# The first four cells of a fused mLSTM and feed-forward kernel: exponents by bias, scaling on GpSimd, and cell 4 turned within the first product group

## The chip, the cores and the metric

The kernel runs on one core of one Trainium2 chip. The metric is the device time of one execution in microseconds; before the change the median of three runs is 540.57 us (540.18 to 541.71). The profile is of one further execution, whose span is 539.1 us.

## The reference

An mLSTM cell goes over 768 time steps for 4 batches and 8 heads with head dimension 40; its output, seen as 3072 rows of 320, goes through a feed-forward block whose activation is h times cos(h). All in float32.

```python
for t in range(S):
    m_new = np.maximum(f_gate[:, :, t] + m, i_gate[:, :, t])
    f_stab, i_stab = np.exp(f_gate[:, :, t] + m - m_new), np.exp(i_gate[:, :, t] - m_new)
    C = f_stab * C + i_stab * outer(vt, kt);  n = f_stab * n + i_stab * kt     # per batch and head
    y[:, :, t] = sigmoid(o_gate) * (C @ qt) / np.maximum(np.abs(n @ qt), 1.0)
...
h = x @ w_in            # 3072x320 by 320x2048
return (h * np.cos(h)) @ w_out
```

## The kernel before

**Tiling.** Time is cut into 6 chunks of 128 steps; with 4 batches that makes N = 24 *cells*, numbered n = 4c + b. Within a cell the recurrence is written as attention with decay. `turn` transposes q and k on TensorE and `turn_out` copies them out of PSUM. `scores` multiplies them, and `weigh` (VectorE, L451) multiplies the scores by E, the decay matrix of 128 x 1024. `values` multiplies the result by v, giving ph. `normalize` divides by the denominator (dn, L533 to L535), multiplies by the gate (y, L538) and writes the scaled z in the order of the feed-forward (L542 and L546). `seam` transposes z on TensorE into px and forms the cell's contribution pu to the state (with kw from `weigh_k`, k weighed by gates on GpSimd, L392). `seam_out` copies px to xT and `state` adds pu to the state, both on ScalarE for the first four cells.

**E.** It is exp of minus (M spread over rows, minus a per-row number from `tab`), masked to the lower triangle. `decay_exponents` subtracts on VectorE (L370) and masks on GpSimd (L371) before `decay` takes the exponential on ScalarE in one instruction (L379). `decay_by_bias` (L381 to L387) instead gives ScalarE the per-row number as bias, which takes one instruction for each of the 8 heads (L385), and masks on GpSimd afterwards (L386). Cells 0 and 1 have a third way, by products on TensorE (`wall_in`, `spread`, `decay_exponents_half`).

**Staging.** `first_cells` (L760 to L872) writes out by hand the order of the first four cells, which have no feed-forward beside them. The order of a call in the program is its order in the queue of its engine: each of TensorE, VectorE, ScalarE, GpSimd and the queue of transfers on SyncE works strictly through its own list. Then `both_parts(c, b)` runs for every chunk c and batch b: the feed-forward of chunk c in eight `Up` groups (h for 256 columns of w_in, and cosine by range reduction and ScalarE's Sin) and `down` groups, with the cells of chunk c + 1 between them. The first `Up` needs xT of all four cells, so it follows `seam_out(3)`.

**Weights.** The weights come as 8-byte floats and are turned to float32 in pieces: `parts` on ScalarE (L138, L140), `join` on VectorE (L144, L146, L148) with a last addition on GpSimd (L149), or on VectorE where a caller says so. The first three pieces are joined within `first_cells`.

**Fillers.** `warm(k)` issues k products of a zero tile, 128 x 512 in bfloat16, which keep TensorE active.

**Buffers.** z and y have one buffer each. In PSUM, cells 0 and 2 use a ring of two buffers (`ps_a`), cells 1 and 3 one of four (`ps_o`).

**The gates.** `gates_first` computes the running maximum M0 of the first chunk and writes it to DRAM (L223); `load_E(2)` and `load_E(3)` read it back, spread over 128 rows, and stand in the queue of SyncE behind that write. `gates_less_sums` (L242) subtracts 32 x 640 elements for the later chunks, ahead of the scan in `gates_maxima` (L247).

Of the kernel before, what the change touches and what calls it, by code (L numbers as in the profile page):

```python
# [16 lines left out]
OP = mybir.AluOpType  # L17
# [12 lines left out]
def kernel(  # L30
# [20 lines left out]
    nc = tc.nc  # L51
# [165 lines left out]
    def gates_first():  # L217
        nc.vector.tensor_tensor_scan(out=F0, data0=one.to_broadcast([BH, C]), data1=F0, initial=0.0,
                                     op0=OP.mult, op1=OP.add)
        nc.vector.tensor_tensor(out=a0, in0=a0, in1=F0, op=OP.subtract)  # L220
        nc.vector.tensor_tensor_scan(out=M0, data0=one.to_broadcast([BH, C]), data1=a0, initial=-1.0e30,
                                     op0=OP.mult, op1=OP.max)
        nc.gpsimd.dma_start(out=M_d[0], in_=M0)  # L223
        nc.vector.tensor_scalar(out=nM, in0=M0[:, C - 1:C], scalar1=-1.0, scalar2=None, op0=OP.mult)
        nc.scalar.activation(out=e0, in_=a0, func=AF.Exp, bias=nM)

    def gates_first_out():
        pg = ps_o.tile([128, 2, BH], FP, name="pg", tag="o")
        for j, src in enumerate((a0, e0)):
            nc.tensor.transpose(pg[:, j], src, ident[0:BH, 0:BH])  # L230
        nc.vector.tensor_copy(out=tab[:, 0, 0:2], in_=pg)
# [7 lines left out]
        nc.vector.tensor_tensor_scan(out=flat[0], data0=flat[3], data1=flat[0], initial=0.0, op0=OP.mult, op1=OP.add)  # L239

    def gates_less_sums():
        nc.vector.tensor_tensor(out=a1, in0=a1, in1=F1, op=OP.subtract)  # L242
        nc.vector.tensor_copy(out=shift[:, 0, 0:1], in_=F0[:, last])
        nc.vector.tensor_copy(out=shift[:, 1:R, 0:1], in_=F1[:, 0:R - 1, last])

# [92 lines left out]
    def load_E(n):  # L338
        c, b = divmod(n, B)
        E = p4.tile([128, H, C], FP, name="E", tag="E")  # L340
        if n not in SPREAD:
            src = M_d[0][ts(b, H)] if c == 0 else M_d[1][ts(b, H), ts(c - 1, C)]
            nc.sync.dma_start(out=E, in_=src.unsqueeze(0).to_broadcast([128, H, C]))
        Es[n] = E
# [33 lines left out]
    def decay(n):  # L378
        nc.scalar.activation(out=Es[n], in_=Es[n], func=AF.Exp, scale=-1.0)  # L379
# [9 lines left out]
    def weigh_k(n):  # L389
        if n < N - B:  # L390
            kw = p2.tile([128, H, D], FP, name="kw", tag="kw")
            nc.gpsimd.tensor_tensor(out=kw, in0=ks[n % NB][:, :, 0:D], in1=cols(n, 1, D), op=OP.mult)  # L392
            kws[n] = kw
# [128 lines left out]

    def normalize(n):
        c, b = divmod(n, B)
        pq, hs = heads_of[n]
        if n >= B:
            ph = hs
            hs = p1.tile([128, H, D1], FP, name="hs", tag="hs")
            nc.vector.tensor_tensor(out=hs, in0=pq, in1=cols(n, 2, D1), op=OP.mult)
            nc.vector.tensor_tensor(out=hs, in0=hs, in1=ph, op=OP.add)  # L530
        dn = p2.tile([128, H], FP, name="dn", tag="dn")

        nc.vector.scalar_tensor_tensor(out=dn, in0=hs[:, :, D], scalar=-TWO_PI, in1=least, op0=OP.mult, op1=OP.max)  # L533
        nc.vector.scalar_tensor_tensor(out=dn, in0=hs[:, :, D], scalar=TWO_PI, in1=dn, op0=OP.mult, op1=OP.max)
        nc.vector.reciprocal(out=dn, in_=dn)  # L535
        y = p1.tile([128, H, D], FP, name="y", tag="y")
        o = sig[c][:, ts(b, DM)].rearrange("t (h d) -> t h d", h=H)
        nc.vector.tensor_tensor(out=y, in0=o, in1=hs[:, :, 0:D], op=OP.mult)  # L538

        z = p1.tile([128, DM + 64], FP, name="z", tag="z")  # L540
        za = z[:, 0:NK * 128].rearrange("t (i k d) -> t k i d", i=2, k=HP)
        nc.vector.tensor_tensor(out=za, in0=y[:, :, 0:DA].rearrange("t (k i) d -> t k i d", i=2),  # L542
                                in1=dn.rearrange("t (k i) -> t k i", i=2).unsqueeze(3).to_broadcast([128, HP, 2, DA]),
                                op=OP.mult)
        shape = [128, 2, H, DL]
        nc.vector.tensor_tensor(out=z[:, NK * 128:].rearrange("t (e h d) -> t e h d", e=2, h=H),  # L546
                                in0=y[:, :, DA:D].unsqueeze(1).to_broadcast(shape),
                                in1=dn.unsqueeze(1).unsqueeze(3).to_broadcast(shape), op=OP.mult)
        ys[n] = z
# [51 lines left out]
    class Up:  # L601


        def __init__(self, c, f2):
            self.c, self.f2 = c, f2
            self.pu = [ps_u.tile([128, B * C], FP, name="pup", tag="up") for _ in range(2)]

            def x(i, r=slice(0, 128)):
                return xT[c][r, i].rearrange("p b t -> p (b t)")

            for i in range(NK):
                for e, pu in enumerate(self.pu):
                    nc.tensor.matmul(pu, w_in_sb[:, i, ts(block(f2, e), 128)], x(i), start=(i == 0), stop=False)  # L613
            for e, pu in enumerate(self.pu):
                r = slice(64 * e, 64 * e + 64)
                nc.tensor.matmul(pu, w_in_l[r, f2], x(NK, r), start=False, stop=True)  # L616
            self.n = [p3.tile([128, B * C], I32, name="n", tag="n") for _ in range(2)]
# [137 lines left out]
    def warm(k, bank=None):  # L755

        for _ in range(k):
            nc.tensor.matmul(bank or pw, nil, nil.unsqueeze(1).to_broadcast([128, HP, 128]), start=True, stop=True)

    def first_cells():  # L760
        nc.vector.memset(nil, 0.0)
        gates_in()
        nc.scalar.copy(out=ident_b, in_=ident)
        load(0, "qk")
        later_gates_in()
        load(1, "qk")
        load(0, "v")
        load_o(0, (0, 1))
        load(2, "qk")
        load_E(0)  # L770
        load_E(1)
        warm(12)
        wall_in(0, 0, pmu)
        wall_in(0, 1, psum_o())
        gates_first()
        gates_first_out()
        spread(0, 0)
        decay_exponents_half(0, 0)
        turn(0)
        turn_out(0, False)  # L780
        gates_sums()
        spread(0, 1)
        decay_exponents_half(0, 1)
        decay(0)
        weigh_k(0)
        load_E(2)
        load(1, "v")
        load(3, "qk")
        load_o(0, (2, 3))
        load_E(3)  # L790
        load(2, "v")
        load(3, "v")
        pieces.extend(weights_in(0))
        wall_in(1, 0, psum_o())
        wall_in(1, 1, psum_o())
        gates_less_sums()
        spread(1, 0)
        decay_exponents_half(1, 0)
        scores(0)
        gates_maxima()  # L800
        turn(1)
        weigh(0)
        sigmoid(0, slice(0, 2))
        turn_out(1, False)
        spread(1, 1)
        decay_exponents_half(1, 1)
        gates_exponents()
        decay(1)
        weigh_k(1)
        values(0)  # L810
        normalize(0)
        scores(1)
        gates_exp()
        turn(2)
        turn_out(2, False)
        warm(2)
        seam(0)
        weigh(1)
        seam_out(0)
        state(0)  # L820
        load(B)
        decay_exponents(2)
        gates_diagonal()
        decay(2)
        weigh_k(2)
        values(1)
        load_E(B)
        load_o(1, (0,))
        load_E(B + 1)
        outs.append((0, weights_out(0)))  # L830
        normalize(1)
        scores(2)
        turn(3)
        sigmoid(0, slice(2, 4))
        seam(1)
        weigh(2)
        decay_exponents(3)
        turn_out(3)
        seam_out(1)
        values(2)  # L840
        decay(3)
        weigh_k(3)
        state(1)
        normalize(2)
        scores(3)
        pg = gates_turn()
        warm(1)
        seam(2)
        weigh(3)
        join(*parts(*pieces.pop(0)))  # L850
        pieces.extend(weights_in(1))
        load(B + 1)
        outs.extend((p, weights_out(p)) for p in range(1, 3))
        load_o(1, (1, 2, 3))
        seam_out(2)
        join(*parts(*pieces.pop(0)))
        state(2)
        gates_keep(*pg)
        values(3)
        normalize(3)  # L860
        turn(B)
        warm(3)
        seam(3)
        join(*parts(*pieces.pop(0)), nc.vector)
        seam_out(3)
        decay_exponents(B)
        load_E(B + 2)
        state(3)
        turn_out(B, False)
        decay(B)  # L870
        weigh_k(B)
        sigmoid(1, slice(0, 1))  # L872
# [17 lines left out]
    def both_parts(c, b):  # L890
# [6 lines left out]
        begin = c == b == 0  # L897
        more = cell and n + 1 < N
        f2 = 2 * b
        up = Up(c, f2)  # L900
        if cell:
            scores(n)
            if begin:
# [144 lines left out]
```

## Time and profile before

| | |
|---|---|
| time, median of 3 | 540.57 us |
| TensorE (PE) busy | 529.1 us, 98% of the span |
| VectorE (DVE) busy | 368.6 us, 68% |
| ScalarE (ACT) busy | 262.1 us, 49% |
| GpSimd (POOL) busy | 166.9 us, 31% |
| transpose of z of cell 0 / 1 / 2 / 3 begins | 19.04 / 23.98 / 29.48 / 37.02 us |
| transposes of q and k of cell 4 begin | 33.80 us |
| first / second `Up` begins | 38.52 / 49.16 us |

The busy shares are averages over the whole span. The change lies in the first 45 us, so the rows of the timeline matter more: a start in us from the beginning of the span, a duration, the engine, the line, what is written and read, and in brackets how long the engine had been idle and for what. PEclk is the share of full clock that TensorE was granted.

### The profile page before, as it was taken

Reading aid. Unit: us, or ns where it says so; the run is one execution under the profiler, and the core shown is the slowest. Engines: PE = TensorE matmul, PEld = TensorE weight load, DVE = VectorE, ACT = ScalarE, POOL = GpSimd, SP = SyncE. Lnnn points to the kernel's source line nnn. Section 1 sums busy time; section 2 is a strip of 40 time slices with the busy share of each in tenths; the row PEclk is TensorE's granted clock in tenths of the full one; section 3 lists DMA queues with packets and bytes.
Section 4 is the critical chain, followed back from the end, with each engine's and each line's share of the span. In section 5 each row is a group of like instructions: output and inputs, shape, how many; then the busy total and the mean of one; then the engine's idle time right before and its main releaser. Section 6 shows DMA issues by size and latency. Waiting matters only on the chain.

```text
span 539.1 us, 9945 instructions
## 1 busy us (share of the span) xinstructions
PE 529.1 (98%) x3635; PEld 334.4 (62%) x3635; DVE 368.6 (68%) x727; ACT 262.1 (49%) x415; POOL 166.9 (31%) x304
## 2 busy tenths in 40 slices
PE   9989899999999999999999999999999999999997
PEld 6865556665566666656656656756656656656555
DVE  5876987968777767777767777776876765522323
ACT  4868695866543436525427425327335332322312
POOL 5531333426353652322422422322222221212121
PEclk9979999999999999999999999999999999999999
DMA  9999996744166744076724075635065000010001
GB/s 140 207 203 217 252 234 174 155 115 83 47 141 144 157 97 84 23 165 143 153 76 107 4 183 139 143 83 117 5 158 117 21 16 11 6 49 0 2 0 49
DMA packets 134512, 56.86 MB, mean 105 GB/s; under 512 B 72080, under 2 KB 130528, under 8 KB 134464
## 3 DMA queue, kind: packets, MB, share of 16 engines
q1 hardware_dynamic: 134320, 56.04, 46.8%
q8 instruction: 28, 0.46, 0.4%
q0 software_dynamic: 96, 0.18, 0.2%
q14 instruction: 20, 0.16, 0.1%
q10 hardware_dynamic: 48, 0.02, 0.0%
HBM read 50.00 MB, written 6.21 MB: 104 GB/s over the span
## 4 chain that ended last, share of the span: by engine, by line
PE 85%; DVE 4%; SPq 4%; DMA 4%; POOL 1%; ACT 1%; issue 1%; DVEq 0%; POOLq 0%
PE po L689 32%; PE pup L613 29%; PE pup L616 9%; PE po L746 4%; PE hp L488 3%; PE ps L445 3%; PE hp L482 2%; SPq L129 1%; PE pu L580 1%; DMA bits<-in_moe_w_in_dram 1%; DMA o<-in_o_gate_dram 1%; SPq L327 1%; DMA qs<-in_q_dram 1%; DVE wt L146 1%; PE pt L426 1%; DMA M_d<-M_rows 1%
## 5 line engine op out<-in xcount | busy, mean ns | idle before, releaser
L613 PE MATMUL pup<-xT,w_in_sb 128*128 128x512 f32 x384 | 175.6, 600 | 0.9 <-POOL w_in_sb L149 0.6
L621 ACT ACTIVATE n<-pup 128x512 int32<-128x512 f32 x96 | 52.1, 594 | 213.4 <-PE pup L616 213.4
L624 DVE SCALAR_TENSOR_TENSOR n<-pup,n 128x512 f32<-128x512 f32 x96 | 61.8, 686 | 119.9 <-ACT n L621 119.9
L689 PE MATMUL po<-w_out_sb,g 128*128 128x320 f32 (+1 forms) x480 | 118.6, 396 | 0.0
L613 PEld LDWEIGHTS pup<-xT,w_in_sb 128*128 128x128 f32 x384 | 70.0, 191 | 73.9 <-issue 61.9
L689 PEld LDWEIGHTS po<-w_out_sb,g 128*128 128x128 f32 x480 | 83.5, 190 | 36.7 <-issue 9.1
L672 POOL TENSOR_TENSOR sg<-g 128x128 f32<-128x128 f32 x80 | 36.6, 457 | 192.7 <-DVE g L633 191.2
L629 ACT ACTIVATE n<-n 128x512 f32<-128x512 f32 x96 | 58.8, 630 | 12.1 <-DVE n L624 12.1
L633 DVE SCALAR_TENSOR_TENSOR g<-pup,n 128x512 f32<-128x512 f32 x96 | 61.7, 685 | 2.5 <-ACT n L629 1.2
L616 PE MATMUL pup<-xT,w_in_l 64*128 64x512 f32 x192 | 54.2, 641 | 0.0
L371 POOL TENSOR_SCALAR_AFFINE_SELECT E<-E 128x1024 f32<-128x1024 f32 x19 | 20.7, 1091 | 104.4 <-DVE E L370 83.4
L689 PE MATMUL po<-T,sg 128*128 128x160 f32 x240 | 39.4, 300 | 0.0
L746 PE MATMUL po<-w_out_sb,g 128*128 128x320 f32 x128 | 36.6, 439 | 1.3 <-POOL w_out_sb L149 1.0
L616 PEld LDWEIGHTS pup<-xT,w_in_l 64*128 64x128 f32 x192 | 14.4, 184 | 36.4 <-issue 35.6
L689 PEld LDWEIGHTS po<-T,sg 128*128 128x128 f32 x240 | 34.8, 190 | 0.2
L451 DVE TENSOR_TENSOR E<-ps,E 128x512 f32<-128x512 f32 x48 | 30.7, 680 | 5.6 <-PE ps L445 5.6
L410 DVE STREAM_TRANSPOSE t<-qs 128x512 f32<-128x512 f32 x32 | 32.8, 1101 | 0.0
L445 PEld LDWEIGHTS ps<-t,t 40*128 40x128 f32 (+1 forms) x384 | 25.0, 188 | 9.7 <-issue 8.9
L746 PEld LDWEIGHTS po<-w_out_sb,g 128*128 128x128 f32 x128 | 23.7, 190 | 11.0 <-POOL w_out_sb L149 1.3
L379 ACT ACTIVATE E<-E 128x1024 f32<-128x1024 f32 x21 | 22.2, 1058 | 16.9 <-POOL E L371 15.7
L445 PE MATMUL ps<-t,t 40*128 40x128 f32 (+1 forms) x384 | 25.8, 274 | 0.0
L370 DVE TENSOR_TENSOR E<-E,tab 128x1024 f32<-128x1024 f32 x19 | 23.1, 1215 | 0.5 <-DMA E<-M_d 0.5
(146 smaller groups left out, 647.2 us busy)
## 6 DMA issues: line engine op xcount, KB each, us to landing
E<-M_d SPq DMA_DIRECT2D x22, 512.0 KB
bits<-in_moe_w_in_dram SPq DMA_DIRECT2D x40, 128.0 KB
bits<-in_moe_w_out_dram SPq DMA_DIRECT2D x8, 640.0 KB
room<-G_d SPq DMA_DIRECT2D x32, 128.0 KB
ks<-in_k_dram SPq DMA_DIRECT2D x24, 160.0 KB
vs<-in_v_dram SPq DMA_DIRECT2D x24, 160.0 KB
qs<-in_q_dram SPq DMA_DIRECT2D x32, 80.0 KB
qs<-in_k_dram SPq DMA_DIRECT2D x32, 80.0 KB
```

The costliest lines, as they stand in the source:

```text
L410: nc.vector.transpose(out=dst.rearrange("r p (t x) -> r p x t", x=T4), in_=src.rearrange("r p (x d) -> r p x d", x=T4)[:, :, :, 0:32])
L445: nc.tensor.matmul(ps[j][:, p], kT[r, p], qT[r, p], start=True, stop=True)
L451: nc.vector.tensor_tensor(out=w, in0=pss[n][j], in1=w, op=OP.mult)
L613: nc.tensor.matmul(pu, w_in_sb[:, i, ts(block(f2, e), 128)], x(i), start=(i == 0), stop=False)
L616: nc.tensor.matmul(pu, w_in_l[r, f2], x(NK, r), start=False, stop=True)
L621: nc.scalar.activation(out=self.n[e], in_=self.pu[e], func=AF.Copy, bias=0.25)
L624: nc.vector.scalar_tensor_tensor(out=self.n[e].bitcast(FP), in0=self.pu[e], scalar=0.25, in1=self.n[e], op0=OP.add, op1=OP.subtract)
L629: nc.scalar.activation(out=r, in_=r, func=AF.Sin, scale=TWO_PI_DOWN)
L633: nc.vector.scalar_tensor_tensor(out=g, in0=self.pu[e], scalar=TWO_PI, in1=self.n[e].bitcast(FP), op0=OP.mult, op1=OP.mult)
L672: nc.gpsimd.tensor_tensor(out=S[:, i], in0=x, in1=y, op=op)
L689: nc.tensor.matmul(out, g, w, start=(f2 == 0 and first), stop=end, skip_group_check=True)
L746: nc.tensor.matmul(po[c][b], gs[c, f][:, ts(b, C)], w_out_sb[:, f], start=(f == 0), stop=(f == NF - 1))
```

## The change

It concerns what is done before and within the first `Up`. At the head, three zero products of twelve go, and the products that prepare E of cell 0 come after the transposes of the first gates; M0 is written from ScalarE's queue in place of GpSimd's. To take work off VectorE, the subtraction of `gates_less_sums` and the two z instructions of cells 0, 1 and 2 move to GpSimd, and cells 2 and 3 get their exponentials with the bias on ScalarE in place of the subtraction on VectorE. Cell 4's transposes, with all that follows from them, move from before `seam(3)` to the middle of the first `Up`, after its first four products; six zero products stand where three stood. Some loads change places in SyncE's queue.

```diff
 gates_first:
-        nc.gpsimd.dma_start(out=M_d[0], in_=M0)
+        nc.scalar.dma_start(out=M_d[0], in_=M0)
 gates_less_sums:
-        nc.vector.tensor_tensor(out=a1, in0=a1, in1=F1, op=OP.subtract)
+        nc.gpsimd.tensor_tensor(out=a1, in0=a1, in1=F1, op=OP.subtract)
 normalize:
+        last = nc.gpsimd if n < B - 1 else nc.vector
-        nc.vector.tensor_tensor(out=za, ...
+        last.tensor_tensor(out=za, ...
-        nc.vector.tensor_tensor(out=z[:, NK * 128:]...
+        last.tensor_tensor(out=z[:, NK * 128:]...
 Up.__init__(self, c, f2, between=None):
             for i in range(NK):
+                if i and between:
+                    between()
 first_cells:
-        warm(12)
+        warm(9)
+        gates_first()
+        gates_first_out()
         wall_in(0, 0, pmu)
         wall_in(0, 1, psum_o())
-        gates_first()
-        gates_first_out()
...
         weigh_k(0)
+        load(1, "v")
         load_E(2)
-        load(1, "v")
         load(3, "qk")
         load_o(0, (2, 3))
+        load(2, "v")
         load_E(3)
-        load(2, "v")
...
         load(B)
-        decay_exponents(2)
         gates_diagonal()
-        decay(2)
+        decay_by_bias(2)
         weigh_k(2)
         values(1)
...
         normalize(1)
         scores(2)
         turn(3)
         sigmoid(0, slice(2, 4))
         seam(1)
         weigh(2)
-        decay_exponents(3)
         turn_out(3)
         seam_out(1)
         values(2)
-        decay(3)
+        decay_by_bias(3)
         weigh_k(3)
         state(1)
         normalize(2)
...
         join(*parts(*pieces.pop(0)))
+        seam_out(2)
+        join(*parts(*pieces.pop(0)))
         pieces.extend(weights_in(1))
...
-        seam_out(2)
-        join(*parts(*pieces.pop(0)))
         state(2)
+        last = parts(*pieces.pop(0))
         gates_keep(*pg)
         values(3)
         normalize(3)
-        turn(B)
-        warm(3)
+        warm(6)
         seam(3)
-        join(*parts(*pieces.pop(0)), nc.vector)
+        join(*last, nc.vector)
         seam_out(3)
-        decay_exponents(B)
         load_E(B + 2)
         state(3)
+
+    def cell_after_first():
+        turn(B)
         turn_out(B, False)
+        decay_exponents(B)
         decay(B)
         weigh_k(B)
         sigmoid(1, slice(0, 1))
 both_parts:
-        up = Up(c, f2)
+        up = Up(c, f2, cell_after_first if begin else None)
```

More of the change, by code (lines that the diff above doesn't have):

```diff
@@ L541, in normalize @@
         za = z[:, 0:NK * 128].rearrange("t (i k d) -> t k i d", i=2, k=HP)
-        nc.vector.tensor_tensor(out=za, in0=y[:, :, 0:DA].rearrange("t (k i) d -> t k i d", i=2),
+        last.tensor_tensor(out=za, in0=y[:, :, 0:DA].rearrange("t (k i) d -> t k i d", i=2),
                                 in1=dn.rearrange("t (k i) -> t k i", i=2).unsqueeze(3).to_broadcast([128, HP, 2, DA]),
@@ L545, in normalize @@
         shape = [128, 2, H, DL]
-        nc.vector.tensor_tensor(out=z[:, NK * 128:].rearrange("t (e h d) -> t e h d", e=2, h=H),
+        last.tensor_tensor(out=z[:, NK * 128:].rearrange("t (e h d) -> t e h d", e=2, h=H),
                                 in0=y[:, :, DA:D].unsqueeze(1).to_broadcast(shape),
@@ L601, with __init__ @@
     class Up:
-        def __init__(self, c, f2):
+        def __init__(self, c, f2, between=None):
             self.c, self.f2 = c, f2
```

## The prediction

> **What bounds the kernel now.** I read the page's busy shares first, then its 40 slices, then the timeline of the first 50 us engine by engine, and last the waits.
>
> ```profile
> PE 529.1 (98%) x3635; PEld 334.4 (62%) x3635; DVE 368.6 (68%) x727; ACT 262.1 (49%) x415; POOL 166.9 (31%) x304
> ...
> PEclk9979999999999999999999999999999999999999
> ```
>
> TensorE is busy throughout, so time is won only by starting the run of `Up` groups sooner. One early slice has a low clock. The waits of TensorE sum to only about 6 us, and after the second `Up` none is for a transfer, so I let a shift of that `Up` (49.16 us) carry to the end one for one. The timeline around cell 4's transposes, which the change moves:
>
> ```profile
> 30.33 1.98 PE L470 MATMUL ph<-vs,E 128*128 128x41 f32 x16
> 33.80 1.09 PE L426 MATMUL pt<-ident,qs 128*128 128x128 f32 x4 [1.49 <-DMA qs<-in_q_dram]
> 34.86 1.09 PE L426 MATMUL pt<-ident,ks 128*128 128x128 f32 x4
> 35.74 1.48 PE L758 MATMUL pw<-nil 128*128 128x512 bf16 x3
> 37.02 0.84 PE L573 MATMUL px<-ident,z 128*128 128x128 f32 x3
> ```
>
> TensorE waits 1.49 us for q of cell 4; the table by stretches gives clock 1.00 for 30 to 33 us, 0.50 for 33 to 39.8 and 1.00 after. So a short wait costs twice: four transposes take 1.09 us here and 0.60 elsewhere. Earlier the rows to watch are ScalarE's and GpSimd's:
>
> ```profile
> 20.16 0.59 ACT L594 COPY st<-pu 40x164 f32<-40x164 f32 x2
> 21.83 1.06 ACT L379 ACTIVATE E<-E 128x1024 f32<-128x1024 f32 x1 [1.08 <-POOL E L371]
> 22.90 1.28 ACT L308 ACT_TABLE_LOAD   x1
> ...
> 25.44 0.49 ACT L588 COPY xT<-px 128x384 f32<-128x384 f32 x1
> 25.94 1.28 ACT L379 ACT_TABLE_LOAD   x1
> 27.24 1.06 ACT L379 ACTIVATE E<-E 128x1024 f32<-128x1024 f32 x1
> ```
>
> GpSimd's rows beside them:
>
> ```profile
> 20.71 1.09 POOL L371 TENSOR_SCALAR_AFFINE_SELECT E<-E 128x1024 f32<-128x1024 f32 x1 [1.97 <-DVE E L370]
> 21.77 0.72 POOL L392 TENSOR_TENSOR kw<-ks,tab 128x320 f32<-128x320 f32 x1
> ```
>
> And the biased exponentials of a later cell:
>
> ```profile
> 74.71 2.45 ACT L385 ACTIVATE E<-E,tab 128x128 f32<-128x128 f32 x8
> ```
>
> GpSimd has done cells 2 and 3's masks well before they are needed, and ScalarE is nearly solid; the last row prices the biased form: 2.45 us for 8 against 1.06 for one.
>
> **What the Trainium skill says.** "TensorE: Matmul & The Clock Gate", Part 1: an idle array drops to half clock, decided in free-running windows of about 3.4 us. The trace agrees: the drop at 33.0 and the release at 39.8 are 6.8 us apart, two windows, and the head's zero products are 0.43 us apart but 0.21 from about 5.7 us, eight windows before 33.0. "SBUF — State Buffer", "Who interferes with whom": GpSimd and VectorE share a port pair and the later one blocks. Agrees: `join`'s first instruction takes 1.13 us beside a GpSimd addition, 0.42 alone. "ScalarE: Activation LUTs", "What ACT_TABLE_LOAD costs": 1283 ns; the trace has 1283.
>
> **The change, part by part.**
>
> *Head.* Three zero products at 0.427 us are 1.28 us, but the two 128x512 products behind them then run at half clock and the gate transposes too; they end near 6.0 instead of 6.7. I take 0.7 us (0.2 to 1.2: the window's phase differs by run).
>
> *M0's write.* On ScalarE it costs an issue of 0.42 us ahead of the 0.40 us exponential, ready by 4.8, under the ninth product's end (1.12 + 9 x 0.427 = 4.96). SyncE's wait for the write was 0.6 us and its queue is slowed by transfers anyway: 0 to 0.6 us for loads, and nothing in the new order waits for them. The other reorderings of loads: 0, since E(2) and E(3) were never waited for.
>
> *Subtraction to GpSimd.* 1.26 us (the 32x640 row L254) for 0.80, while GpSimd is idle from 8.65 to 13.8; the scan behind it comes about 1 us sooner. ScalarE however is solid from 10.61 (cell 0's exponential) to 18.99 (copy of cell 2's q, which frees the PSUM buffer that px(0) takes), so px(0) gains only the head's 0.7: 19.04 becomes 18.3.
>
> *z on GpSimd.* Rows of two-operand GpSimd work: 128 columns 0.457, 320 columns 0.72, so 256 is about 0.62 and both z instructions about 1.0 us (0.9 to 1.2) for VectorE's 0.70. VectorE gets 3 x 0.7 plus 2 x 1.22 (L370) back, 4.5 us, but in 20 to 28 us it was itself waiting for ph. What counts is the queue: GpSimd's order becomes mask(2), kw(2), z(1), mask(3), kw(3), z(2), and a mask must now wait for all 8 exponentials. On TensorE `seam(1)` stands ahead of `values(2)`, `seam(2)` ahead of `values(3)`, so they wait for z.
>
> *Cell 2.* In before, ScalarE ended `state(0)` 1.7 us after px(0) began. So exponentials begin 18.3 + 1.7 = 20.0 and end 22.45; mask 1.09 to 23.55; kw to 24.25; z(1) to 25.25. px(1) at 25.3 against 23.98: 1.3 later. TensorE ended `turn(3)` near 23.5 and stands 1.8 us.
>
> *Cell 3.* `seam_out(1)` ends 1.07 after px(1) (as cell 0's did): 26.35; table load 1.28 to 27.65 (the sigmoid before it is unmoved); exponentials to 30.1; mask 31.2; kw 31.9; z(2) 32.9. px(2) at 32.95 against 29.48: 3.5 later, after another wait of about 2 us.
>
> *To px(3).* px(2) and pu(2) 0.85 and ph 1.98, as in before: 35.8. VectorE: weigh(3) to 31.2 + 1.28 = 32.5; first join 1.6 to 34.1, its GpSimd addition 1.27 to 35.4. The second piece's `parts` follow `seam_out(2)` at 34.0, first half 34.6; VectorE's L144 is blocked by that addition to 35.65, the rest 1.2 to 36.85; `normalize(3)` took 1.98 (34.02 to 36.00): z(3) at 38.8. So px(3) at 38.8, or 37.8 if the join does not stand in the way. Before it was 37.02. Six zero products (1.3 us, from 35.8) are hidden in this.
>
> *First `Up` with cell 4 inside.* From px(3), at full clock: 1.1 to the first product (xT copied), 8 rows of 0.43 = 3.45, transposes 0.9, L616 0.96, scores 0.95: weigh(4) at 7.4. From weigh to the second `Up` before took 49.16 - 44.88 = 4.3. Sum 11.7 against 12.14 before, which was partly cold. ScalarE: cell 4's copies, exponential and sigmoid (table 1.28) end at 7.4, so `near` fits ahead of the weigh's end; nothing more is exposed. Removed: the wait of 1.49 and 3.2 us of transposes and zero products before px(3).
>
> *Clock.* Two waits of about 2 us are longer than the one that dropped it before. Cold rows are about 1.5 to 2 times longer; on the part from px(3) on I take 1.1 us of loss, between 0 and 3.
>
> Sum: second `Up` at 38.8 + 11.7 + 1.1 = 51.6, 2.4 later than 49.16: 543.0 us.
>
> **The rivals.**
>
> *A, likeliest, 0.45:* as above, 543.0, slower. For it: order in the queues and rows that are all measured.
>
> *B, 0.13: the same waits but the clock stays full.* 38.8 + 11.7 = 50.5, +1.3: 541.9, within 0.3%. Against it: the drop at 33.0 after only 0.67 us of idleness.
>
> *C, 0.25: relief of VectorE pays and GpSimd isn't the bound.* If z came as early as on VectorE, all comes 0.7 sooner, ph(3) ends at 31.6; the second piece of weights (31.05, ScalarE waited 0.5 us for it) then bounds: VectorE's join and `normalize(3)` end near 35.6, px(3) there, second `Up` at 47.3: -1.9, 538.7, faster. For it: VectorE 5.00 of 5 us busy in 10 to 15 and 4.66 in 25 to 30, and the wait of 1.49 us gone. Against it: the sum for z(1).
>
> *D, 0.17: cold from cell 3 to the first `Up`.* ph(3) 1.4 longer to 37.2, six zero products at 0.427 to 39.8 = px(3); 11.7 plus 0.6 (px, pu) and 1.7 (a window of `Up` at half): 53.8, +4.6: 545.2.
>
> **How the numbers follow.** A and D are slower by over 0.3% (1.6 us): 0.62. B is within: 0.13. C is faster: 0.25. Time from A, 543.0. The range runs from just under C, 538.0, to just over D, 545.5; it takes in the head's 0.2 to 1.2, z's 0.9 to 1.2 and the clock's 0 to 3.
>
> **What would show it.** After: px(1) starts near 25.3 with a TensorE wait of 1 to 2 us for GpSimd's z, px(2) near 33 with another; the biased exponentials 2.45 us; GpSimd's mask of cell 3 near 30; the first half-clock stretch starts before 33 us. I am wrong if TensorE's px rows wait for nothing, if z(1) is done before 24 us, or if the second `Up` starts before 49 us.

## The result and the profile after

| | before | after |
|---|---|---|
| time, median of 4 runs each | 540.93 us | 547.62 us |
| ratio, 95% interval | | 1.0126, 1.0087 to 1.0165 |
| span of the profiled run | 539.1 us | 545.6 us |
| px of cell 0 / 1 / 2 / 3 begins | 19.04 / 23.98 / 29.48 / 37.02 | 21.47 / 28.02 / 35.85 / 43.33 us |
| second `Up` begins | 49.16 | 55.68 us |

The changed kernel is slower by 6.7 us. The forecast had the side, but the measured loss is nearly three times its 2.4 us, and the time lies above the range.

The page of the changed kernel: busy times, and the clock in 40 slices.

```profile
PE 533.5 (98%) x3635; PEld 338.3 (62%) x3635; DVE 365.0 (67%) x718; ACT 264.7 (49%) x429; POOL 171.1 (31%) x310
PEclk9968999999999999999999999999999999999999
```

VectorE did 3.6 us less in all, as the change meant it to, and TensorE has its low-clock slice again, one tenth lower. The whole loss is made before the second `Up`: it starts 6.52 us later and the span is 6.5 us longer. TensorE's rows at the head, in the kernel before:

```profile
5.96 0.38 PE L350 MATMUL pmu<-wall,ident_b 128*128 128x512 bf16 x1
6.17 0.38 PE L350 MATMUL pm<-wall,ident_b 128*128 128x512 bf16 x1
6.48 0.24 PE L230 MATMUL pg<-ident,a 32*128 32x32 f32 x1
6.57 0.22 PE L230 MATMUL pg<-ident,e 32*128 32x32 f32 x1
6.72 1.16 PE L357 MATMUL pmu<-M_rows,ident 128*128 128x128 f32 x8
```

and in the changed kernel:

```profile
5.07 0.31 PE L230 MATMUL pg<-ident,a 32*128 32x32 f32 x1
6.89 0.31 PE L230 MATMUL pg<-ident,e 32*128 32x32 f32 x1 [1.51 <-ACT e L225]
7.13 0.61 PE L350 MATMUL pmu<-wall,ident_b 128*128 128x512 bf16 x1
7.53 0.63 PE L350 MATMUL pm<-wall,ident_b 128*128 128x512 bf16 x1
7.96 1.91 PE L357 MATMUL pmu<-M_rows,ident 128*128 128x128 f32 x8
```

ScalarE's there, in the kernel before:

```profile
4.11 0.40 ACT L225 ACTIVATE e<-a,nM 32x128 f32<-32x128 f32 x1 [1.26 <-DVE nM L224]
```

and in the changed one:

```profile
6.00 0.39 ACTq L223 DMA_DIRECT2D M_d<-M_rows  x1
6.44 0.40 ACT L225 ACTIVATE e<-a,nM 32x128 f32<-32x128 f32 x1 [3.59 <-DMA ks<-in_k_dram]
```

M0 was ready at 3.7 us, yet its write was issued at 6.00, after a transfer of k of cell 0 had landed. The exponential e0 stands behind it on ScalarE, TensorE's second gate transpose waits for e0, and everything on TensorE stands behind that. After the 1.51 us the products still run at half speed (0.40 us apart where before had 0.21, and 1.91 us where it had 1.16). The clock column of the profile gives 1.00 there all the same, so at the head only the durations show it. The profile has one more instruction of ScalarE for that line, a wait on a semaphore, ahead of the write:

```profile
L223 ACTq EVENT_SEMAPHORE  x1: 17/17/17, 5.9 to 5.9; - x1
```

Which semaphore it is stands in the compiled program, not in the profile. Its instructions, with names shortened and with what they wait for:

```
ACT  L223 EventSemaphore          [waits DMAHW3_49]
ACT  L223 DMACopy M_d<-M0_rows    [waits DVE_49]
ACT  L225 Activation e0<-a0,nM    [waits DVE_49]
```

A completion semaphore is a counter that a transfer raises when it has landed. In this program the transfers issued by SyncE and ScalarE take eight of them in turn (DMAHW0 to DMAHW7), and M0's write got DMAHW3, which the transfer of k of cell 0 had before it and was still using. GpSimd's transfers have eight of their own (DMASW0 to DMASW7).

GpSimd's rows of the changed kernel, for the cells 2 and 3:

```profile
25.62 1.09 POOL L386 TENSOR_SCALAR_AFFINE_SELECT E<-E 128x1024 f32<-128x1024 f32 x1 [4.02 <-ACT E L385]
26.68 0.72 POOL L392 TENSOR_TENSOR kw<-ks,tab 128x320 f32<-128x320 f32 x1
27.36 0.61 POOL L543 TENSOR_TENSOR z<-y,dn 128x256 f32<-128x256 f32 x1
27.94 0.40 POOL L547 TENSOR_TENSOR z<-y,dn 128x128 f32<-128x128 f32 x1
33.07 1.09 POOL L386 TENSOR_SCALAR_AFFINE_SELECT E<-E 128x1024 f32<-128x1024 f32 x1 [4.73 <-ACT E L385]
```

and TensorE's rows that wait for them or follow:

```profile
28.02 0.69 PE L574 MATMUL px<-ident,z 128*128 128x128 f32 x3 [1.57 <-POOL z L543]
...
35.85 0.85 PE L574 MATMUL px<-ident,z 128*128 128x128 f32 x3
36.63 0.78 PE L581 MATMUL pu<-vs,kw 128*40 128x41 f32 x16
37.34 3.64 PE L470 MATMUL ph<-vs,E 128*128 128x41 f32 x16
40.77 2.76 PE L761 MATMUL pw<-nil 128*128 128x512 bf16 x6
43.33 0.81 PE L574 MATMUL px<-ident,z 128*128 128x128 f32 x3
```

This is the predicted queue: mask behind eight exponentials, kw, then z, and TensorE waits. The table by stretches (us, TensorE busy, clock, then two columns of transfers) says what it did to the clock:

```profile
26.20:29.60 3.40, 1.82 (x27) 1.00 0.99 220
29.60:33.00 3.40, 3.40 (x28) 0.61 1.29 148
33.00:36.40 3.40, 3.40 (x23) 0.50 1.08 234
36.40:39.80 3.40, 3.40 (x30) 0.50 1.08 323
39.80:43.20 3.40, 3.40 (x12) 0.50 1.04 232
43.20:46.60 3.40, 3.18 (x25) 0.88 0.46 133
```

It is at half from about 30.3 to 44 us, twice as long as before. The second wait for z is not even visible: the slow products fill it. The values of cell 3 take 3.64 us for 1.98, and the six zero products 2.76 for 1.47.

### The profile page after: what moved, and what is told of

It reads as the page before. It is cut to its first block, busy times and chain, and to the rows that moved or that the text cites. A ratio compares the mean times of both kernels' runs of the same rounds, so it can differ in the third digit from the quotient of the medians.

```text
span 545.6 us, 9959 instructions
## 1 busy us (share of the span) xinstructions
PE 533.5 (98%) x3635; PEld 338.3 (62%) x3635; DVE 365.0 (67%) x718; ACT 264.7 (49%) x429; POOL 171.1 (31%) x310
## 4 chain that ended last, share of the span: by engine, by line
PE 86%; DVE 7%; issue 2%; POOL 1%; SPq 1%; ACT 1%; DMA 1%; DVEq 0%; ACTq 0%; POOLq 0%
PE po L692 31%; PE pup L616 29%; PE pup L619 9%; PE po L749 4%; PE ps L445 3%; PE hp L488 3%; PE hp L482 2%; PE ph L470 1%; PE pu L581 1%; DVE wt L146 1%; SPq L327 1%; DVE wt L148 1%; DVE n L627 1%; DMA ks<-in_k_dram 1%; DVE g L636 1%
## 5 line engine op out<-in xcount | busy, mean ns | idle before, releaser
L371 POOL TENSOR_SCALAR_AFFINE_SELECT E<-E 128x1024 f32<-128x1024 f32 x17 | 18.6, 1094 | 98.7 <-DVE E L370 77.7
L379 ACT ACTIVATE E<-E 128x1024 f32<-128x1024 f32 x19 | 20.1, 1058 | 15.7 <-POOL E L371 14.4
```

## The experiments

Each kernel differs from the changed one ("after") or from the one before by the edit shown, and each time is a median set beside the median of the kernel before on the same chip (540.66 to 540.98 us). Where a time is called less than that of after (547.62 us), the two medians can come from different chips. None leaves out a part of the computation.

### Parts of the changed kernel undone

**M0's write back on GpSimd.**

```diff
-        nc.scalar.dma_start(out=M_d[0], in_=M0)
+        nc.gpsimd.dma_start(out=M_d[0], in_=M0)
```

> The changed kernel with M0's write back in GpSimd's queue, nothing else. Theory H (on ScalarE the write waited for the transfer of ks of cell 0, which landed at 5.9 us, and held the exponential e0 and so TensorE behind it): the second gate transpose starts near 5.1 in place of 6.89 us, px of cell 0 near 18.5 to 19.0 in place of 21.47, and the time falls by 2.4 to 3.0 us, to about 545. Rival W (nine zero products are too few, so the clock is released late whatever is behind them): px of cell 0 stays above 20.5 us and the time falls by less than 1 us.

Measured: 545.56 us, ratio to before 1.0087 (1.0070 to 1.0105), so 2.1 us less than after. The gain is only just clear of the spread: the interval overlaps that of after (1.0087 to 1.0165), and the slowest of these four executions, 546.00 us, lies at the fastest of after, 546.01.

**M0's write on ScalarE, behind e0.**

```diff
-        nc.scalar.dma_start(out=M_d[0], in_=M0)
         nc.vector.tensor_scalar(out=nM, ...
         nc.scalar.activation(out=e0, ...
+        nc.scalar.dma_start(out=M_d[0], in_=M0)
```

> The changed kernel with M0's write still in ScalarE's queue, but behind e0 in place of ahead of it. Theory H: as good as taking the write off ScalarE, 2.4 to 3.0 us less than the changed kernel, since only what stands behind the waiting write is held, and the next work of ScalarE is at about 8 us. If the write itself, coming late to DRAM, or ScalarE's queue of transfers were the cause: no gain, px of cell 0 stays near 21.5 us.

Measured: 545.25 us, ratio 1.0083 (1.0066 to 1.0100), 2.4 us less than after; all four executions (545.12 to 545.31) are below the fastest of after. TensorE's rows:

```profile
5.04 0.24 PE L230 MATMUL pg<-ident,a 32*128 32x32 f32 x1
5.12 0.22 PE L230 MATMUL pg<-ident,e 32*128 32x32 f32 x1
...
18.96 0.52 PE L574 MATMUL px<-ident,z 128*128 128x128 f32 x3 [0.83 <-ACT t L432]
```

The second transpose is at 5.12 in place of 6.89 and px of cell 0 at 18.96 in place of 21.47. The write on ScalarE's queue is harmless in itself; what it holds is the instruction behind it.

But px of cell 0 is no sooner than the 19.04 of the kernel before, and the reason is another wait. The sigmoid of cell 0's gate o stands on ScalarE behind cell 0's exponential. Its first row, a table load, in the kernel before:

```profile
11.71 1.28 ACT L308 ACT_TABLE_LOAD   x1
```

and here:

```profile
11.74 1.28 ACT L308 ACT_TABLE_LOAD   x1 [0.78 <-DMA o<-in_o_gate_dram]
```

Before, the exponential ended at 11.67, and o was there. Here it ends at 10.96, and ScalarE waits for the transfer of o. Five other profiles in which the exponential is early show the same wait (0.75 to 1.23 us), and none of them has px of cell 0 before 18.84 us.

In the kernel with the write on GpSimd, px of cell 0 came at 19.83, later than expected: TensorE waited 0.74 us for E of cell 0 and was then at half clock from 15.9 to 19.3 us. That E was late since VectorE was held up, here by the subtraction on GpSimd; its rows in that kernel:

```profile
9.65 0.13 DVE L243 COPY room<-F 32x1 f32<-32x1 f32 x1
9.71 1.47 DVE L244 COPY room<-room 32x4 f32<-32x4 f32 x1
```

A copy of four columns takes 1.47 us instead of 0.15, beside the subtraction on GpSimd (9.63 to 11.16), and the scan behind it gains nothing from the 0.80 us that were moved away.

**z of cells 0 to 2 back on VectorE.**

```diff
-        last = nc.gpsimd if n < B - 1 else nc.vector
+        last = nc.vector
```

> The changed kernel with z of cells 0 to 2 back on VectorE; exponentials still by bias. Theory Z (z stands on GpSimd behind the mask, and the mask behind eight exponentials, so TensorE waits for z): from px of cell 0 to px of cell 1 falls from 6.55 to about 5 us, from there to px of cell 2 from 7.83 to about 6, and the time falls by 3 to 5 us, to 543 to 544.5. Rival S (ScalarE with its 2 x 1.39 us of additional exponentials is the bound itself): these two intervals stay above 6.0 and 7.3 us and the time falls by less than 1.5 us.

Measured: 544.29 us, ratio 1.0063 (1.0044 to 1.0082), 3.3 us less than after. The first interval falls to 4.93 us (21.32 to 26.25), the second only to 7.22.

**Both:** z on VectorE and M0's write on GpSimd.

> Both undone: M0's write on GpSimd and z on VectorE. Theories H and Z: the two gains add, 5.5 to 8 us less than the changed kernel, 539.6 to 542, so all of the loss of 6.7 us is explained by these two edits. Rivals W and S: more than 3 us of the loss stays, 543.5 or above.

Measured: 544.30 us, ratio 1.0069 (1.0052 to 1.0085), no better than z on VectorE alone. The gains do not add; 3.4 us of the loss stay. So the theory that these two edits make all of it fell. The rows of TensorE and, below, of ScalarE show what had stood behind z:

```profile
31.67 0.79 PE L272 MATMUL pd<-F,one 32*128 32x128 f32 x2 [1.37 <-ACT st L595]
```

```profile
27.40 1.28 ACT L385 ACT_TABLE_LOAD   x1
28.69 2.44 ACT L385 ACTIVATE E<-E,tab 128x128 f32<-128x128 f32 x8
31.05 0.58 ACT L595 COPY st<-pu 40x164 f32<-40x164 f32 x2
```

With z out of the way, the eight exponentials of cell 3 hold the copy of cell 1's state on ScalarE, that copy holds a PSUM buffer, and TensorE waits 1.37 us for the buffer.

### Parts of the change alone, on the kernel before

**M0's write on ScalarE,** with twelve zero products.

```diff
-        nc.gpsimd.dma_start(out=M_d[0], in_=M0)
+        nc.scalar.dma_start(out=M_d[0], in_=M0)
```

> The kernel before with only M0's write moved to ScalarE's queue. Theory H: the write waits until about 5.9 us for the transfer of ks of cell 0, e0 ends near 6.85, and the second gate transpose starts near 6.9 instead of 6.57; since twelve zero products and two products still stand ahead of it, the clock is released as before and the loss is small, 0.3 to 0.8 us (541.2 to 541.7). If the write costs the same 2 us with twelve as with nine products: 542.5 or above.

Measured: 540.21 us, ratio 0.9990 (0.9978 to 1.0003). The second gate transpose starts at 6.85 and waits for little: the twelve products end late enough to cover the held exponential. px of cell 0 is 0.45 us later in the profile (19.49), but in the times not even the small loss is there.

**z on GpSimd.**

```diff
+        last = nc.gpsimd if n < B - 1 else nc.vector
-        nc.vector.tensor_tensor(out=za, ...
+        last.tensor_tensor(out=za, ...
-        nc.vector.tensor_tensor(out=z[:, NK * 128:]...
+        last.tensor_tensor(out=z[:, NK * 128:]...
```

> The kernel before with only z of cells 0 to 2 moved to GpSimd; exponents as before, so the masks are done early. Theory Z+S (z is late only because the mask ahead of it waits for eight exponentials): z of cell 1 at 23.05 to 24.1, px of cell 1 within 0.3 us of 23.98, px of cell 2 within 0.4 of 29.48, time within 0.6 us of before. If GpSimd is simply too slow for z: px of cell 1 over 0.8 us later and the time over 1 us longer.

Measured: 540.69 us, ratio 0.9995 (0.9983 to 1.0007). GpSimd's rows:

```profile
20.50 1.09 POOL L371 TENSOR_SCALAR_AFFINE_SELECT E<-E 128x1024 f32<-128x1024 f32 x1 [0.66 <-DVE E L370]
21.56 0.72 POOL L392 TENSOR_TENSOR kw<-ks,tab 128x320 f32<-128x320 f32 x1
23.67 0.61 POOL L543 TENSOR_TENSOR z<-y,dn 128x256 f32<-128x256 f32 x1 [1.39 <-DVE y L539]
```

Here mask and kw are done and GpSimd waits for y. z costs 1.0 us on GpSimd and nothing on the way to the end.

**Exponentials by bias.**

```diff
-        decay_exponents(2)
-        decay(2)
+        decay_by_bias(2)
...
-        decay_exponents(3)
-        decay(3)
+        decay_by_bias(3)
```

> The kernel before with only the exponentials of cells 2 and 3 by bias; z on VectorE. Theory S (ScalarE's exponentials hold state(1), and with it a PSUM buffer that TensorE needs after cell 3's scores): px of cell 1 within 0.5 us of 23.98, state(1) ends near 30.5 in place of 28.8, px of cell 2 near 31, and since cell 4's q comes only at 33.7 part of it is hidden: time plus 0.8 to 2.5 us, 541.7 to 543.4. If biased exponentials cost nothing without z on GpSimd: within 0.5 us of before.

Measured: 542.89 us, ratio 1.0047 (1.0033 to 1.0062), inside the expected 0.8 to 2.5 us. The profile, though, shows another course than the expected one: the clock was at half in 22 to 28 us after a wait of 0.88 us ahead of px of cell 0, px of cell 1 came at 25.86, and the buffer was free in time. Common to both courses is that cell 3's E comes late (weigh, join and z of VectorE follow it), and TensorE then waits 2.66 us for z of cell 3. How much of the 1.9 us is the bias and how much the clock is not settled.

**z and bias together:** the last two diffs.

> The kernel before with z of cells 0 to 2 on GpSimd and the exponentials of cells 2 and 3 by bias, nothing else. Alone, z cost nothing and the bias about 2 us. Theory Z+S (they meet in GpSimd's queue: mask behind eight exponentials, z behind the mask): from px of cell 0 to px of cell 1 about 6.5 us and from there to px of cell 2 about 7.7 us, as in the changed kernel; time 3.5 to 5.5 us over before, 544.4 to 546.4. If the effects only add: about 543, the intervals no longer than with the bias alone.

Measured: 545.23 us, ratio 1.0075 (1.0047 to 1.0103), 4.6 us over the kernel before; the parts alone gave 0 and 1.9. The interval overlaps that of the bias alone, but none of these four executions (544.37 to 546.28) is below any of its seven (542.40 to 544.37). TensorE's rows:

```profile
19.15 0.52 PE L574 MATMUL px<-ident,z 128*128 128x128 f32 x3 [0.49 <-ACT t L432]
...
25.70 0.70 PE L574 MATMUL px<-ident,z 128*128 128x128 f32 x3 [1.57 <-POOL z L543]
...
33.16 0.90 PE L574 MATMUL px<-ident,z 128*128 128x128 f32 x3 [1.14 <-POOL z L543]
34.70 3.64 PE L470 MATMUL ph<-vs,E 128*128 128x41 f32 x16
```

Intervals of 6.55 and 7.46 us, both waits, and the slow values of cell 3: the changed kernel's middle, without its head. The two edits meet in one queue.

**The changed head.** M0's write on ScalarE with nine zero products and the gate transposes ahead of the products for E.

```diff
-        warm(12)
+        warm(9)
+        gates_first()
+        gates_first_out()
         wall_in(0, 0, pmu)
         wall_in(0, 1, psum_o())
-        gates_first()
-        gates_first_out()
...
-        nc.gpsimd.dma_start(out=M_d[0], in_=M0)
+        nc.scalar.dma_start(out=M_d[0], in_=M0)
```

> The kernel before with the head of the changed kernel: nine zero products, the products for E of cell 0 behind the gate transposes, M0's write on ScalarE. With twelve products M0's write alone cost nothing. Theory H: with nine, TensorE stands still from 5.4 to about 6.9 us and the clock is released late; px of cell 0 near 20.5 to 21.5, time 1.5 to 2.5 us over before, 542.4 to 543.5. If the write is harmless in itself and the loss of the changed head came from GpSimd's subtraction: within 0.7 us of before.

Measured: 541.98 us, ratio 1.0009 (0.9994 to 1.0025): 1.3 us by the medians, not told from nothing by the ratio. TensorE stands still as expected (1.42 us), but in the profiled execution the products behind the wait ran at full speed at once, and there was no half-clock stretch at all. That execution is not typical: it is one of four in 20 whose mean granted clock is 1.000, and these took 539.07 to 539.35 us; the other 16 have 0.986 to 0.997 and took 540.26 to 543.48.

Over all profiles with nine zero products the theory does better. The eight products behind the gate transposes take 1.91 us in three of the four kernels in which TensorE stood still there (1.05 in this one), and 1.05 to 1.36 us in the six in which it did not. So the wait makes a late release more likely, not certain. A window of the clock that begins at another moment in each run would make such a difference; that is argued, not shown.

**Cell 4 in the first `Up`, six zero products.**

```diff
-        turn(B)
-        warm(3)
+        warm(6)
         seam(3)
...
-        decay_exponents(B)
...
+    def cell_after_first():
+        turn(B)
         turn_out(B, False)
+        decay_exponents(B)
         decay(B)
...
```

> The kernel before with only cell 4's transposes moved into the first Up group and six zero products in place of three. My account of that part: px of cell 3 starts when VectorE has done its join and z, near 36.0 in place of 37.02, and the second Up begins 11.7 to 12.4 us later: 47.8 to 48.5 against 49.16, so 0.6 to 1.4 us faster, 539.5 to 540.3. If the move is what costs (cell 4's exponents and sigmoid now late for the second Up): slower than before.

Measured: 542.03 us, ratio 1.0017 (1.0005 to 1.0029): slightly slower, a miss. px of cell 3 comes sooner, at 35.66, yet after a wait, and then the clock goes:

```profile
35.66 0.52 PE L573 MATMUL px<-ident,z 128*128 128x128 f32 x3 [1.96 <-DVE z L542]
...
36.84 3.51 PE L615 MATMUL pup<-xT,w_in_sb 128*128 128x512 f32 x4 [0.22 <-ACT xT L588]
```

The four products take 3.51 us where full clock takes 1.96, and the second `Up` starts at 49.26 where it did before. The transposes of cell 4 had filled time in which VectorE was joining weights ahead of z.

### What remained: exponents as before

**The changed kernel with the old exponents in cells 2 and 3.**

```diff
-        decay_by_bias(2)
+        decay_exponents(2)
+        decay(2)
...
-        decay_by_bias(3)
+        decay_exponents(3)
+        decay(3)
```

> The changed kernel with the exponents of cells 2 and 3 as before (VectorE, mask, one exponential); z still on GpSimd. Alone on the kernel before, z cost nothing, the bias 0.5% and both together 0.75%. Theory Z+S: with the masks early again z on GpSimd is harmless here too; px of cell 0 to px of cell 1 near 5 us (6.55 in the changed kernel), on to px of cell 2 near 5.5 (7.83); 3.5 to 5 us less than the changed kernel, 542.6 to 544. If something else in the changed kernel makes z late, both intervals stay above 6 us.

Measured: 541.55 us, ratio 1.0016 (1.0003 to 1.0030): 6.1 us less than after, more than expected. The second interval is 5.19 us; the first is 6.40, but z was done in time (25.1 to 26.1), and its products ran at half clock. px of cell 3 begins at 38.80, against 43.33.

**And M0's write on GpSimd.**

> As the previous kernel of this job, with M0's write on GpSimd too. Theory H: a further 1.5 to 2.4 us less, 540.5 to 542. If the head's loss depended on the late exponentials behind it: the same as the previous kernel within 0.7 us.

Measured: 541.93 us, ratio 1.0033 (1.0021 to 1.0045). No gain, against 2.1 us with the biased exponentials. In this profile the clock fell both before px of cell 0 and at the first `Up` (3.59 us for its four products).

**And the subtraction on VectorE.**

```diff
-        nc.gpsimd.tensor_tensor(out=a1, in0=a1, in1=F1, op=OP.subtract)
+        nc.vector.tensor_tensor(out=a1, in0=a1, in1=F1, op=OP.subtract)
```

> As the previous kernel of this job, with the subtraction of the later chunks' gates back on VectorE. In the profiles of the changed head a copy of 32x4 elements on VectorE took 1.08 to 1.47 us beside that subtraction on GpSimd in place of 0.15. If the subtraction costs on the way to px of cell 0: px of cell 0 0.4 to 0.8 us sooner and the time 0.3 to 1 us less. If ScalarE hides it: the same within 0.3 us.

Measured: 541.85 us, ratio 1.0019 (1.0008 to 1.0030), the same within 0.1 us. px of cell 0 begins at 18.96 in place of 20.28 us, more than expected, and the wait of 0.73 us ahead of cell 0's values is down to 0.16; but in this profile the clock fell from about 29 us on, and the time is the same. What comes early in this stage is lost again to the next wait.

This last kernel still has the reordered loads, which were not tried alone. Its 0.19% over the kernel before is no more than cell 4's move costs alone (0.17%), so nothing shows that they cost or gain anything.

### A better order

**best1: joins behind z, cell 4 in the first `Up`.** On the kernel before:

```diff
-        join(*parts(*pieces.pop(0)))
+        second = parts(*pieces.pop(0))
         state(2)
+        third = parts(*pieces.pop(0))
         gates_keep(*pg)
         values(3)
         normalize(3)
-        turn(B)
-        warm(3)
+        warm(6)
         seam(3)
-        join(*parts(*pieces.pop(0)), nc.vector)
+        join(*second)
+        join(*third, nc.vector)
```

with `turn(B)` and what follows it within the first `Up`, as in the change.

> The kernel before with cell 4 in the first Up and six zero products, and the VectorE half of the joins of the second and third piece of weights behind z of cell 3 in place of ahead of it. With the joins ahead, TensorE waited 1.96 us for z and the clock fell. Now z of cell 3 follows ph directly: px of cell 3 at 33.5 to 34.5, no half-clock stretch after it, second Up near 46, so 2 to 3.5 us faster than before, 537.5 to 539. If the second piece, joined later, holds the first Up: no more than 0.5 us faster.

Measured: 540.84 us, ratio 1.0003 (0.9991 to 1.0015). The first half went as expected: px of cell 3 at 34.16, the first `Up` at full clock. Then

```profile
47.36 5.27 PE L615 MATMUL pup<-xT,w_in_sb 128*128 128x512 f32 x8 [1.46 <-DVE g L635]
```

the second `Up` waits for the gate, because ScalarE has cell 4's late exponential, a table load and the sigmoid ahead of its first step; the clock falls and eight rows take 5.27 us for 3.70.

**best2: nine zero products and the gate transposes first.** It is best1 with the first part of the diff of the changed head, M0's write on GpSimd.

> As the previous kernel of this job, with nine zero products and the gate transposes ahead of the products for E of cell 0, M0's write still on GpSimd. Theory H says that the head without the write on ScalarE gains 0.2 to 1.2 us over twelve products: 536.5 to 538.5. If nine are too few in themselves: slower than the previous kernel by over 0.5 us.

Measured: 540.77 us, ratio 1.0000 (0.9983 to 1.0016), another miss. px of cell 0 at 19.02: what the head gained is waited for again (1.37 us for ScalarE's copy of cell 2's q, after ScalarE had waited 1.23 us for o).

**best3: best1 with the sigmoid behind the sines.**

```diff
     def cell_after_first():
...
         weigh_k(B)
-        sigmoid(1, slice(0, 1))
 both_parts:
         sums(c, f2)
+        if begin:
+            sigmoid(1, slice(0, 1))
```

> The kernel best1 with the sigmoid for cell 4 behind the sines of the first Up in place of ahead of their first step. In best1 the second Up waited 1.46 us for VectorE's gate, since ScalarE came to the first step late, behind a table load and the sigmoid, and the clock then fell. Without that: no wait over 0.5 us ahead of the second Up, which starts near 46 us; 1.5 to 3 us faster than before, 537.7 to 539.3. If ScalarE's mask-bound exponential of cell 4 is what holds it: within 0.5 us of before.

Measured: 539.67 us, ratio 0.9985 (0.9970 to 1.0001). The wait ahead of the second `Up` is 0.32 us and it runs at full clock (3.70 us). By the median 1.0 us faster than before, but the interval just touches 1, so a gain is not shown, and it is less than expected. The second `Up` started at 48.67, not near 46: in this profile the clock fell after px of cell 0, and px of cell 3 came at 36.62.

## Why the prediction was right on the side and wrong on the size

By its own steps; what each adds to the start of the second `Up`:

| step | predicted | measured |
|---|---|---|
| px of cell 0 | 18.3 | 21.47 us |
| to px of cell 1 | 7.0 | 6.55 |
| to px of cell 2 | 7.65 | 7.83 |
| to px of cell 3 | 5.85 | 7.48 |
| to the second `Up` | 11.7 + 1.1 | 12.35 |
| second `Up` | 51.6 | 55.68 us |

**The head: the step that failed.** The prediction had M0's write on ScalarE "ready by 4.8, under the ninth product's end", and the head 0.7 us sooner. Both terms were wrong, and together they put px of cell 0 2.43 us later than before in place of 0.7 sooner: 3.2 us of the error of 4.1 at the second `Up`.

The larger is the write. The prediction took its issue for 0.42 us and put the wait in front of it at nothing. The exponential was ready at 6.84; with nine zero products nothing covers that, and the products behind it ran at half speed. Moving the write behind e0, or back to GpSimd, takes 2.4 and 2.1 us off the changed kernel. But twelve products hide the same wait in the times, and the 2.1 us are not there with z on VectorE (544.29 with the write on ScalarE, 544.30 on GpSimd) nor with the old exponents (541.55 and 541.93). So it is a loss of that combination, not of the edit alone.

The other is the 0.7 us itself. The prediction saw that ScalarE was solid from cell 0's exponential on, and let the whole row move forward with the head. It overlooked that the sigmoid behind that exponential waits for o, which came at 11.7 to 12.0 us with the old head and with the new: with the write out of the way px of cell 0 came at 18.96, so the head had nothing to win.

**The subtraction.** It was to bring the scan about 1 us sooner. It brought nothing, since VectorE's next copy took 0.9 to 1.3 us longer beside it, and 0.15 us again with the subtraction back on VectorE; the prediction named the shared ports and did not apply them here. ScalarE waited 0.46 us for the gates behind it.

**z on GpSimd, cells 2 and 3.** Right in mechanism and size: 6.55 and 7.83 against 7.0 and 7.65 us, the eight exponentials 2.44 us (2.45), z 1.0 us, the wait 1.57 us. "What counts is the queue" is shown: z alone costs nothing, the bias alone 1.9 us, both together 4.6 us, and with the old exponents the changed kernel is 6.1 us faster. One reading was wrong without harm: the masks of cells 2 and 3 were not done "well before they are needed". In the rows that the prediction shows, ScalarE waits 1.08 us for cell 2's mask (21.80, exponential at 21.83), and cell 3's ends at 27.18, with its exponential at 27.24. What matters is that a mask which waits for nothing on ScalarE is out of the way before z can start. Rival C, relief of VectorE, is refuted: VectorE did less and then waited for ph and for the masks (7.4 and 2.9 us in the first 80 us).

**The clock: a second term, mis-sized.** A counted loss from px of cell 3 on only. The values of cell 3 took 1.66 us more and the six zero products, meant to be hidden, ended at 43.5 us, after z (42.64): 1.6 us on this step. Rival D had just this course (1.4 us for the values, zero products last, px after them). Its 4.6 us with the head's 3.2 would be 7.8, against 6.5 measured: the slow stretch that it put into the first `Up` did not come. After px of cell 3 the loss was 12.35 - 11.7 = 0.65 us, below the 1.1 taken. That the first two intervals came out although the head was wrong is no luck: with the old head the two edits gave nearly the same ones (6.55 and 7.46 us).

"An idle array" is too strong for what drops the clock here. In the kernel before, TensorE was busy for 2.71 of the 3.40 us ahead of the drop at 33.0; in the changed kernel, for 2.33 of the 3.40 us ahead of its drop near 30.35.

**One for one.** Right: span minus the start of the second `Up` is 489.94 us before, 489.92 after, and between 489.77 and 489.95 in the profiles of the experiments but for those named best1, best2 and best3, which change what follows.

**The chances.** B (clock stays full) did not come. The range ended at D and allowed the head to miss by 0.5 us only; two steps that both can be late must be allowed to be late together.

## What to carry to other kernels

Two moves that relieve a busy engine can be cheap alone (here 0 and 1.9 us) and dear together (4.6 us), if they meet in one engine's queue: write down the order of that queue and put each instruction's last input beside it. A transfer moved to an engine that also computes puts its own wait in front of what stands behind it there; place it after the last urgent instruction. Before an earlier start is counted as a gain, look for the next transfer that the chain waits for. In a stage that fills TensorE loosely, look at the clock after each new wait: time gained at one place here was often lost to the next wait or to a stretch at half clock.

## What the runs showed that was not expected

A copy of 32x4 elements on VectorE took 1.08 us (after) and 1.47 us (with M0's write on GpSimd) beside a GpSimd subtraction, 0.15 us without. The row of the kernel before:

```profile
11.30 0.15 DVE L244 COPY room<-room 32x4 f32<-32x4 f32 x1
```

The subtraction took 1.54 us on GpSimd, not the 1.26 of a like row.

A single kernel's times spread by up to 5.5 us, 1.0%, in these runs (539.61 to 545.10 us for the changed kernel with the old exponents): more than most single edits here are worth, so edits in this stage need many runs to be told apart. Much of the spread goes with the clock. Of 60 executions of the kernel before on one chip, the 3 with a mean granted clock of 1.000 have a mean span of 537.1 us, the 18 with 0.997 have 538.2, and the 15 with 0.994 have 539.3. One stretch of 3.4 us at half clock lowers the mean over 539 us by 0.003 (3.4 x 0.5 / 539), so these are, by estimate, none, one and two such stretches, at about 1 us each. The changed kernel's four executions have 0.984 to 0.987, four or five by the same estimate; its profile shows four. A profile is one draw from this, and is best read beside the clocks of the other runs.
